# A fused attention and bilinear FFN kernel: up weights in three transfers, and batch 0's two up products in a new order

## The chip, the cores and the metric

The kernel runs on one core of a Trainium2 chip. A core has the engines TensorE (PE, with its weight loads PEld), VectorE (DVE), ScalarE (ACT), GpSimd (POOL) and SyncE (SP), and sixteen DMA engines that all queues share. The time is the device time of one execution in microseconds, here the median of several runs; lower is better.

## What is computed

Eight batches of eight heads, 576 tokens each, head size 64, 32 memory slots. Inputs are float32. The reference, cut to what matters:

```python
a = exp(phi - max(phi over tokens))                 # softmax over the tokens, per memory slot
a = a / (sum(a over tokens) + 1e-9)
k_m = einsum('bhsm,bhsd->bhmd', a, k)               # 32 memory keys and values per head
v_m = einsum('bhsm,bhsd->bhmd', a, v)
attn = softmax(q @ k_m.T / 8)                       # 576 x 32 per head
x = (attn @ v_m), heads side by side                # 4608 tokens x 512
out = ((x @ w_a) * (x @ w_b)) @ w_out               # 512 -> 1536 (two up products) -> 512
```

## The kernel before

**One batch.** The attention output is never formed. For a batch, `sums` (L245) makes the memory keys and values from `exp_sb` (exponentials of phi) and `kv_sb` on TensorE, `transpose` (L269) turns them, `scores` (L279) and `exp_scores` (L301) make E, `denominators` (L308) and `normalise` (L317) make A, the normalised attention. `fold` (L327) multiplies the memory values into a strip of an up weight (w_a is x = 0, w_b is x = 1), and `take_fold` (L345 on) casts the result to `vab`, one half on ACT, one on DVE (L349). An up product is then `vab` times A: `up` (L584) computes for a block i of 128 of the 1536 hidden columns, and for the halves of 288 tokens it is given, first `pa` (L592), which ACT copies to `a_sb` (L595), then `pb` (L602), which DVE multiplies with `a_sb` into `ht` (L605). There are 12 blocks; the first four need columns 0 to 512 of the up weights, and so on. The down product takes `ht` and `wo_sb` into the output.

**Order.** The schedule is written out by hand. A string names units; `chain` (L659) runs one after the other, `ups` (L608) runs up products with units from a second string in the slots between them. `ksN` and `vsN` are sums, `ktN` and `vtN` transposes, `qtN` transposes of q on DVE, `sN`, `eN`, `denN`, `nrN` scores to A, `vNa` and `xNa` fold and cast of strip N of w_a (`b`: w_b), `hv` and `hx` the same for strips of 256 columns. `fN` issues N products of a zero tile of 256 columns, of which nothing is used (`fill`, L147). `yN` issues N products of the first four down tiles (`early_downs`, L408), which read the first third of `wo_sb` in their first 16 products, the second third in the next 16, the last third in the last 16. Batch 0 is L671 to L674, batch 1 L675 to L681; from batch 2 on, the down products run as sums of pairs of token tiles (`two_downs`, L453), for which GpSimd makes `w_sums` once (`sum_weights`, L425) and `h_sums` per pair (L444).

**Loads.** Phi of batch 0 comes on SP's queue and half of its k on ACT's; all other loads are issued by GpSimd in program order, since they cast float32 to float16. The order there: q, k and v of batch 0; the up weights in column strips, w_a and w_b by turns (`load_wab`, L98: strips 0 to 256, 256 to 512, 512 to 1024, 1024 to 1536, called at L157 and L165 to L167); then `wo_sb` in thirds, mixed with phi, k, q and v of batch 1 (L168 to L176); then batches 2 and 3. From the ninth such transfer on, each issue waits for the landing of the transfer eight places before it. GpSimd also computes, so its queue holds arithmetic and issues in one order.

**Buffers.** `a_sb` comes from a pool of four (L48). TensorE's results go to eight PSUM banks, taken in turn (`Banks`, L122).

Of the kernel before, what the change touches and what calls it, by code (L numbers as in the profile page):

```python
# [8 lines left out]
F32 = mybir.dt.float32  # L9
F16 = mybir.dt.float16  # L10
AF = mybir.ActivationFunctionType
ALU = mybir.AluOpType

P = 128
# [4 lines left out]
def kernel(  # L19
# [11 lines left out]
    nc = tc.nc  # L31

    B, H, S, D = q.shape
# [6 lines left out]
    HALF = S // 2  # L40
# [7 lines left out]
    apool = ctx.enter_context(tc.tile_pool(name="apool", bufs=4))  # L48
# [43 lines left out]
    def load(b):  # L92
        load_phi(b)
        load_k(b)
        load_v(b)
        load_q(b)

    def load_wab(lo, hi):  # L98
        nc.gpsimd.dma_start(out=wa_sb[:, :, lo:hi], in_=wa_rows[:, :, lo:hi])
        nc.gpsimd.dma_start(out=wb_sb[:, :, lo:hi], in_=wb_rows[:, :, lo:hi])  # L100
# [6 lines left out]
    ht = consts.tile([P, NFF, 2 * S], F16, name="ht")  # L107
# [37 lines left out]
    banks = Banks()  # L145

    def fill(n, cols=512):  # L147

        pw = banks.tile([P, 512], F32, name="pw")
        for _ in range(n):  # L150
            nc.tensor.matmul(pw[:, :cols], warm[:, :P], warm[:, :cols], start=True, stop=True)
# [2 lines left out]
    make_identity(nc, ident)  # L154
    nc.vector.memset(kv_sbs[0][:, 2], 1.0 / CS)
    nc.vector.tensor_copy(out=kvs[0][:, 0, 0:2], in_=k_f32)
    load_wab(0, 256)  # L157

    ones = consts.tile([P, 4, 32], F16, name="ones")
    nc.vector.memset(ones, 1.0)  # L160
# [1 line left out]
                            pattern=[[-32, 4], [0, 32]], channel_multiplier=1)  # L162
    nc.gpsimd.affine_select(out=ones, in_=ones, compare_op=ALU.is_ge, fill=0.0, base=31,
                            pattern=[[32, 4], [0, 32]], channel_multiplier=-1)
    load_wab(256, 512)  # L165
    load_wab(512, 1024)
    load_wab(1024, 1536)  # L167
    load_wo(0)  # L168
# [10 lines left out]
    attn = {}  # L179
    vabs = {}  # L180
# [237 lines left out]
    KH = NFF // 2  # L418
    NH = d_model // 2
    w_sums = wpool.tile([P, 4, KH, NH], F16, name="w_sums")  # L420

    def quarter(x, y):
        return wo_sb[:, KH * x:KH * (x + 1), NH * y:NH * (y + 1)]

    def sum_weights():  # L425
        t = [w_sums[:, x] for x in range(4)]
        for out, in0, in1 in ((t[0], quarter(0, 1), quarter(0, 0)), (t[1], quarter(1, 1), t[0]),
                              (t[2], quarter(1, 1), quarter(0, 1)), (t[3], quarter(1, 0), t[1])):
            nc.gpsimd.tensor_tensor(out=out, in0=in0, in1=in1, op=ALU.subtract)

    def tokens_of(cidx, x):
        pair, c = divmod(cidx, NI)
# [148 lines left out]

    work = Work()

    def up(b, i, hfs):  # L584
        A, vab = attn[b], vabs[b]
        base = S * (b % 2)
        fs = slice(P * i, P * (i + 1))
        a_sbs = []
        for hf in hfs:
            pa = banks.tile([P, HALF], F32, name="pa")  # L590
            for g in range(2):
                nc.tensor.matmul(pa, vab[0][:, g, fs], A[:, g, HALF * hf:HALF * (hf + 1)],  # L592
                                 start=(g == 0), stop=(g == 1))
            a_sb = apool.tile([P, HALF], F16, name="a_sb")
            nc.scalar.copy(out=a_sb, in_=pa)  # L595
            a_sbs.append(a_sb)
        if len(hfs) > 1:
            yield
        for hf in hfs:
            pb = banks.tile([P, HALF], F32, name="pb")  # L600
            for g in range(2):
                nc.tensor.matmul(pb, vab[1][:, g, fs], A[:, g, HALF * hf:HALF * (hf + 1)],  # L602
                                 start=(g == 0), stop=(g == 1))
            t0 = base + HALF * hf
            nc.vector.tensor_tensor(out=ht[:, i, t0:t0 + HALF], in0=a_sbs[hf - hfs[0]], in1=pb, op=ALU.mult)  # L605
        yield

    def ups(steps, side=()):  # L608

        side = iter(side)  # L610
        for step in steps:
            for _ in up(*step):
                work.advance()
                next(side, us[step[0]]["-"])()
        for f in side:
            work.advance()
            f()

    def steps(b, lo, hi):

        return [(b, i, (0, 1)) for i in range(lo, hi)]
# [14 lines left out]
    def slots(b, names):  # L636

        def both(fs):
            return lambda: [f() for f in fs]
        def unit(n):  # L640
            if n == "fin":
                return lambda: work.pull(-work.done % NFF)
            if n == "L":
                return lambda: load(b + 2) if b + 2 < B else None
            if n[0] == "y":
                return lambda: some(int(n[1:]))
            if n[0] == "d" and n[1:].isdigit():
                return lambda: work.pull(int(n[1:]))
            return us[b + n.endswith("'") - n.endswith("_")][n.rstrip("'_")]

        return [both([unit(n) for n in x.split("+")]) for x in names.split()]
# [3 lines left out]
    def some(n):  # L655
        for _ in range(n):
            next(early, None)

    def chain(b, plan):  # L659


        for x in plan.split():
            if x[0] == "f":
                fill(int(x[1:]), 256)
            elif x[0] == "y":
                some(int(x[1:]))
            else:
                us[b][x]()

    fill(16)  # L670
    chain(0, "exp0 exp1 ks0 kt0 qt0 qt1 f2 s0 e0 ks1 kt1 den0 qt2 qt3 f2 s1 nr0 e1 vs0 vs1 den1 vt0 vt1 nr10 nr11 hv0a hx0a")  # L671
    ups(steps(0, 0, 4), slots(0, "hv0b+hx0b hv1a+hx1a - hv1b+hx1b - v1a+x1a - v1b+x1b"))
    load(2)
    ups(steps(0, 4, 12), slots(0, "- - - - v2a+x2a+v2b+x2b - -"))  # L674
    chain(1, "exp0 exp1 y9 ks0 y3 kt0 qt0 qt1 y1 y3 ks1 qt2 s0 e0 y6 kt1 qt3 den0 y3 s1 nr0 e1 y4 y2 den1 vs0 vs1 vt0 y1 vt1 nr1 hv0a hx0a hv0b y3 hx0b y2")  # L675
    load(3)
    sum_weights()
    ups(steps(1, 0, 4), slots(1, "- hv1a+hx1a hv1b+hx1b+y1 - v1a+x1a y3+v1b x1b y3"))
    ups(half_steps(1, 0, 4), slots(1, "- v2a+x2a+v2b+x2b+qt0' - - qt1'+exp0'+qt2' exp1' - kv'+km'+y9"))
# [43 lines left out]
```

The softmax here doesn't subtract the row's maximum and nothing guards it: scores larger than these inputs give would overflow.

## Time and profile before

| | |
|---|---|
| median of 5 runs | 246.93 us (246.54 to 253.03) |
| the profiled execution | 246.93 us |
| its span, first to last instruction | 245.2 us |
| TensorE busy | 232.0 us (95%), 3016 matmuls |
| VectorE, ScalarE, GpSimd busy | 168.8, 158.2, 154.1 us |
| read from HBM, written | 42.47 MB, 9.44 MB |
| mean granted TensorE clock | 0.984 |

Between the span and the time lie 1.7 us outside the first and last instruction. In the profile's timelines a line has the start, the duration, the engine, the line of the kernel, the operation, what it writes and reads, and the count; in brackets stands the idle time before it and what ended it. Matmuls overlap, so the duration of a group is a little longer than its share of the chain. A DMA issue's duration is that of the issuing instruction, not of the transfer. In the chain of waits a line has a start, a length and what the time went to.

### The profile page before, as it was taken

The page shows a single profiled execution, that of the slowest core. Times are in us where ns is not written, and L with a number is a line of the kernel's source. Part 1 is how long each engine was busy: PE and PEld are TensorE (multiplying, and loading weights), DVE is VectorE, ACT ScalarE, POOL GpSimd, SP SyncE. Part 2 cuts the span into 40 slices and gives each one's busy share as a digit, 9 for nine tenths or more (in the row PEclk, how much of TensorE's full clock was granted, in tenths as well). Part 3 has the DMA queues.
Part 4 walks back from the last instruction along what each step waited for, and adds up shares of the span by engine and source line. Part 5 has one row for each costly group of instructions (what it writes and reads, how often), then busy time and mean ns, then how long its engine had stood idle before and what let it go on. Part 6 is the DMA issues. An engine that isn't in the chain of part 4 may idle for free.

```text
span 245.2 us, 7629 instructions
## 1 busy us (share of the span) xinstructions
PE 232.0 (95%) x3016; PEld 165.1 (67%) x3016; DVE 168.8 (69%) x406; ACT 158.2 (65%) x409; POOL 154.1 (63%) x126
## 2 busy tenths in 40 slices
PE   7579899999998999999999999999999999999993
PEld 2234474456655857677787777877787877888882
DVE  3454883568959958876995549866996576756742
ACT  2365672678697489578855858577856867565330
POOL 8733263399899028892898769892849177937001
PEclk9977999999999999999999999999999999999999
DMA  6999999999979803983059832597030303032154
GB/s 198 211 198 206 207 256 207 255 219 283 224 188 205 169 3 102 234 139 88 17 135 223 192 86 43 151 204 167 21 69 3 86 3 87 4 87 54 43 129 119
DMA packets 26099, 33.81 MB, mean 138 GB/s; under 512 B 1968, under 2 KB 20528, under 8 KB 26064
## 3 DMA queue, kind: packets, MB, share of 16 engines
q0 software_dynamic: 19344, 22.84, 50.8%
q1 hardware_dynamic: 6208, 9.70, 15.9%
q10 hardware_dynamic: 512, 0.79, 0.9%
q8 instruction: 23, 0.38, 0.6%
q14 instruction: 12, 0.10, 0.1%
HBM read 42.47 MB, written 9.44 MB: 212 GB/s over the span
## 4 chain that ended last, share of the span: by engine, by line
PE 82%; DMA 11%; DVE 3%; issue 1%; ACT 1%; POOL 1%; DVEq 0%; POOLq 0%
PE pa L592 19%; PE pb L602 18%; PE py L462 16%; PE pv L462 8%; DMA wb_sb<-in_moe_w_b_dram 6%; PE pva L337 5%; PE po L389 5%; DMA kv_sb<-in_v_dram 4%; PE px L462 4%; PE pkv L213 2%; PE pD L314 2%; PE pscore L292 1%; PE pT L242 1%; PE pk L256 1%; POOL q_sb L90 1%
## 5 line engine op out<-in xcount | busy, mean ns | idle before, releaser
L605 DVE TENSOR_TENSOR ht<-a_sb,pb 128x288 f16<-128x288 f16 x192 | 83.0, 449 | 41.8 <-ACT a_sb L595 28.9
L595 ACT CAST a_sb<-pa 128x288 f16<-128x288 f32 x192 | 75.0, 406 | 31.0 <-PE pa L592 29.0
L592 PE MATMUL pa<-A,vab 128*128 128x288 f16 x384 | 76.8, 288 | 1.5 <-DVE A L325 1.1
L602 PE MATMUL pb<-A,vab 128*128 128x288 f16 x384 | 77.2, 289 | 0.8 <-ACT vab L349 0.6
L444 POOL TENSOR_TENSOR h_sums<-ht 128x768 f16<-128x768 f16 x28 | 45.9, 1642 | 38.2 <-DVE ht L605 37.2
L602 PEld LDWEIGHTS <-vab 128*128 128x128 f16 x384 | 37.4, 99 | 13.8 <-issue 1.7
L592 PEld LDWEIGHTS <-vab 128*128 128x128 f16 x384 | 34.6, 98 | 15.7 <-issue 8.5
L462 PEld LDWEIGHTS <-h_sums 128*128 128x128 f16 x384 | 37.4, 98 | 6.9 <-issue 0.4
L349 ACT CAST vab<-pva 128x512 f16<-128x512 f32 (+1 forms) x52 | 28.1, 559 | 12.5 <-PE pva L337 12.5
L349 DVE CAST vab<-pva 128x512 f16<-128x512 f32 (+1 forms) x52 | 32.7, 644 | 2.8 <-PE pva L337 2.1
L462 PEld LDWEIGHTS <-ht 128*128 128x128 f16 x288 | 28.2, 98 | 5.6 <-issue 0.4
L462 PE MATMUL py<-w_sums,h_sums 128*128 128x256 f16 x192 | 30.3, 272 | 0.0
L444 POOL TENSOR_TENSOR h_sums<-h_sums,ht 128x768 f16<-128x768 f16 x14 | 23.1, 1648 | 0.9
L444 POOL TENSOR_TENSOR h_sums<-ht,h_sums 128x768 f16<-128x768 f16 x14 | 23.0, 1642 | 1.0
L305 ACT ACTIVATE E<-pscore 128x288 f16<-128x288 f32 x32 | 11.4, 417 | 11.3 <-PE pscore L292 11.2
L325 POOL TENSOR_TENSOR A<-E,R 128x576 f16<-128x576 f16 x10 | 12.8, 1278 | 7.0 <-ACT R L323 6.7
L462 PE MATMUL pv<-w_sums,h_sums 128*128 128x256 f16 x96 | 16.0, 273 | 0.0
L462 PE MATMUL py<-wo_sb,ht 128*128 128x256 f16 x96 | 16.0, 273 | 0.0
L469 ACT ACTIVATE u<-py 128x256 f32<-128x256 f32 x32 | 12.4, 388 | 5.2 <-PE py L462 4.9
L462 PE MATMUL py<-w_sums,ht 128*128 128x256 f16 x96 | 15.5, 272 | 0.1
L462 PE MATMUL px<-wo_sb,ht 128*128 128x256 f16 x96 | 15.4, 273 | 0.0
L204 DVE STREAM_TRANSPOSE qT<-q_sb 128x288 f32<-128x288 f32 x32 | 14.3, 463 | 1.2 <-DMA q_sb<-in_q_dram 1.2
(64 smaller groups left out, 263.0 us busy)
## 6 DMA issues: line engine op xcount, KB each, us to landing
out_dram<-o_sb SPq DMA_DIRECT2D x68, 128.0 KB, 2.7
kv_sb<-in_v_dram POOLq DMA_DIRECT2D x7, 576.0 KB, 10.7
phi_sb<-in_phi_dram POOLq DMA_DIRECT2D x7, 576.0 KB, 4.6
kv_sb<-in_k_dram POOLq DMA_DIRECT2D x7, 576.0 KB, 8.6
q_sb<-in_q_dram POOLq DMA_DIRECT2D x6, 576.0 KB, 13.4
wo_sb<-in_moe_w_out_dram POOLq DMA_DIRECT2D x3, 512.0 KB, 16.2
q_sb<-in_q_dram POOLq DMA_DIRECT2D x4, 288.0 KB, 13.1
wa_sb<-in_moe_w_a_dram POOLq DMA_DIRECT2D x2, 512.0 KB, 14.4
```

The source lines that it names most:

```text
L204: nc.vector.transpose(out=t["qT"][:, hp, :].bitcast(F32), in_=qs[b][:, hp, :].bitcast(F32))
L325: engine.tensor_tensor(out=attn[b][:, g, sl], in0=t["E"][:, g, sl], in1=t["R", g][:, sl], op=ALU.mult)
L337: nc.tensor.matmul(t["pva", lo, z][g][0][32 * j:32 * j + 32, 0:hi - lo], t["kvT"][64 * r:64 * r + 64, 4 + g, M * j:M * j + M], w_sbs[z][64 ...
L349: engine_copy(out=vabs[b][z][:, g, lo:hi], in_=pva[:, 0:hi - lo])
L389: nc.tensor.matmul(po, ht[:, i, P * c:P * (c + 1)], wo_sb[:, i, :], start=(i == 0), stop=(i == NFF - 1))
L444: engine.tensor_tensor(out=out, in0=in0, in1=in1, op=op)
L462: nc.tensor.matmul(po, lhs[:, i], rhs[:, i], start=first and i == 0, stop=i == KH - 1, skip_group_check=not first)
L469: nc.scalar.mul(out=x, in_=po, mul=scale)
L592: nc.tensor.matmul(pa, vab[0][:, g, fs], A[:, g, HALF * hf:HALF * (hf + 1)], start=(g == 0), stop=(g == 1))
L595: nc.scalar.copy(out=a_sb, in_=pa)
L602: nc.tensor.matmul(pb, vab[1][:, g, fs], A[:, g, HALF * hf:HALF * (hf + 1)], start=(g == 0), stop=(g == 1))
L605: nc.vector.tensor_tensor(out=ht[:, i, t0:t0 + HALF], in0=a_sbs[hf - hfs[0]], in1=pb, op=ALU.mult)
```

## The change

- The up weights come in three transfers each: strips 0 to 512, 512 to 1024, 1024 to 1536.
- `up` is split into `up_half`, one half of one up product; `chain` gets the names `aI` (both halves of block I with w_a) and `bI` (with w_b). Batch 0 is written as two chains with these names: the `a` products of a strip stand up to four blocks ahead of its `b` products.
- For batch 0, `a_sb` lies in the room of `w_sums`, in 20 places instead of four buffers.
- `w_sums` is made in eight operations of half the size instead of four.
- In the first chain of batch 0, the q transposes and the second key sums move ahead, the scores and the ACT steps change places, the second normalise is one piece, and short fills stand between the steps.

Batch 1 and all that follows keep their strings.

```diff
-    load_wab(0, 256)
+    load_wab(0, 512)
...
-    load_wab(256, 512)
     load_wab(512, 1024)
     load_wab(1024, 1536)
...
-            nc.gpsimd.tensor_tensor(out=out, in0=in0, in1=in1, op=ALU.subtract)
+            for x in range(2):
+                sl = slice(KH // 2 * x, KH // 2 * (x + 1))
+                nc.gpsimd.tensor_tensor(out=out[:, sl], in0=in0[:, sl], in1=in1[:, sl], op=ALU.subtract)
...
+    a_sbs = {}
+    spare = w_sums.rearrange("p x i f -> p (x i f)")
+
+    def up_half(b, i, hf, x):
+        ps = banks.tile([P, HALF], F32, name=("pa", "pb")[x])
+        for g in range(2):
+            nc.tensor.matmul(ps, vabs[b][x][:, g, P * i:P * (i + 1)], attn[b][:, g, HALF * hf:HALF * (hf + 1)],
+                             start=(g == 0), stop=(g == 1))
+        if x == 0:
+            if b == 0:
+                n = (2 * i + hf) % 20
+                a_sbs[b, i, hf] = spare[:, HALF * n:HALF * (n + 1)]
+            else:
+                a_sbs[b, i, hf] = apool.tile([P, HALF], F16, name="a_sb")
+            nc.scalar.copy(out=a_sbs[b, i, hf], in_=ps)
+        else:
+            t0 = S * (b % 2) + HALF * hf
+            nc.vector.tensor_tensor(out=ht[:, i, t0:t0 + HALF], in0=a_sbs.pop((b, i, hf)), in1=ps, op=ALU.mult)
...
+            elif x[0] in "ab":
+                i, _, hf = x[1:].partition(".")
+                for h in ([int(hf)] if hf else (0, 1)):
+                    up_half(b, int(i), h, "ab".index(x[0]))
...
-    chain(0, "exp0 exp1 ks0 kt0 qt0 qt1 f2 s0 e0 ks1 kt1 den0 qt2 qt3 f2 s1 nr0 e1 vs0 vs1 den1 vt0 vt1 nr10 nr11 hv0a hx0a")
-    ups(steps(0, 0, 4), slots(0, "hv0b+hx0b hv1a+hx1a - hv1b+hx1b - v1a+x1a - v1b+x1b"))
+    chain(0, "exp0 exp1 qt0 qt1 f12 ks0 f4 kt0 f2 ks1 f1 s0 e0 kt1 qt2 qt3 f2 den0 f4 s1 e1 nr0 f8 vs0 vs1 den1 f2 vt0 vt1 nr1 f4")
+    chain(0, "v0a x0a f4 a0 a1 v0b x0b f4 b0 b1 a2 b2 v1a x1a a3 b3 a4 a5 v1b x1b a6 a7 b4 b5 v2a x2a b6 b7 a8 a9")
     load(2)
-    ups(steps(0, 4, 12), slots(0, "- - - - v2a+x2a+v2b+x2b - -"))
+    chain(0, "v2b x2b a10 a11 b8 b9 b10 b11")
```

## The prediction

> **What bounds the kernel now.** I read the utilisation slices first, then the chain of waits in order of time, then GpSimd's queue, then single transfers. From the page:
>
> ```profile
> DMA  6999999999979803983059832597030303032154
> ```
>
> Each digit is 6.13 us: the 16 DMA engines are 90% busy or more from 6 us to about 67 us. TensorE is busy too, so both must be followed. The chain of waits:
>
> ```profile
> 3.62 10.71 DMA kv_sb<-in_v_dram
> 14.61 15.76 DMA wb_sb<-in_moe_w_b_dram
> 30.41 0.41 PE pva L337 x8
> 30.82 0.60 PE pb L602 x4
> ...
> 36.31 1.94 PE po L389 x9
> ```
>
> Up to 30.41 the start is a queue of loads; the last part of `wb_sb` ends it. Then 11 groups of up products (six pb, five pa, 0.49 each, 5.49 in all), then batch 1's chain, whose gaps the `po` products fill. So it looks as if moving pa groups ahead of the landing must pay. Whether it does depends on what batch 1 waits for. GpSimd's timeline shows how fast the queue drains, since each issue is released by an earlier landing:
>
> ```profile
> 14.61 0.74 POOL L100 DMA_DIRECT2D wb_sb<-in_moe_w_b_dram  x1 [2.06 <-DMA kv_sb<-in_v_dram]
> 16.78 0.74 POOL L104 DMA_DIRECT2D wo_sb<-in_moe_w_out_dram  x1 [1.43 <-DMA wa_sb<-in_moe_w_a_dram]
> 17.84 0.76 POOL L78 DMA_DIRECT2D phi_sb<-in_phi_dram  x1 [0.31 <-DMA wb_sb<-in_moe_w_b_dram]
> 19.15 0.74 POOL L82 DMA_DIRECT2D kv_sb<-in_k_dram  x1 [0.55 <-DMA wa_sb<-in_moe_w_a_dram]
> 20.48 0.70 POOL L90 DMA_DIRECT2D q_sb<-in_q_dram  x1 [0.59 <-DMA wb_sb<-in_moe_w_b_dram]
> 23.09 0.76 POOL L104 DMA_DIRECT2D wo_sb<-in_moe_w_out_dram  x1 [1.91 <-DMA wa_sb<-in_moe_w_a_dram]
> 25.61 0.70 POOL L90 DMA_DIRECT2D q_sb<-in_q_dram  x1 [1.76 <-DMA wb_sb<-in_moe_w_b_dram]
> 28.11 0.70 POOL L85 DMA_DIRECT2D kv_sb<-in_v_dram  x1 [1.80 <-DMA wa_sb<-in_moe_w_a_dram]
> 30.65 0.71 POOL L85 DMA_DIRECT2D kv_sb<-in_v_dram  x1 [1.84 <-DMA wb_sb<-in_moe_w_b_dram]
> 33.25 0.76 POOL L104 DMA_DIRECT2D wo_sb<-in_moe_w_out_dram  x1 [1.90 <-DMA wo_sb<-in_moe_w_out_dram]
> ```
>
> The releases step by 2.17, 1.06, 1.31, 1.33 us for the four 256 KB parts, then by 2.61, 2.52, 2.50, 2.54, 2.60 for 512 KB: a queue in order at a steady pace. Behind the up weights stand batch 1's loads and the rest of `wo_sb`. Two answers of the trace, for batch 1's k (issued at 19.15) and for the three `wo_sb` transfers (issued at 16.78, 23.09, 33.25):
>
> ```profile
> DMA to landing us min/median/max: 18.6/18.6/18.6
> ```
> ```profile
> DMA to landing us min/median/max: 15.4/16.2/18.6
> ```
>
> So k lands at 19.15 + 18.6 = 37.75. In issue order the three lengths are 16.2, 18.6, 15.4: the first must land shortly before it releases the issue at 33.25, and the last before its use at 48.66. So the second third of `wo_sb` lands at 41.7, the last at 48.65. And TensorE uses them here:
>
> ```profile
> 38.18 0.68 PE L256 MATMUL pk<-kv_sb,exp_sb 64*32 64x128 f16 x36
> 41.75 1.46 PE L389 MATMUL po<-wo_sb,ht 128*128 128x512 f16 x6
> 48.66 1.25 PE L389 MATMUL po<-wo_sb,ht 128*128 128x512 f16 x5
> ```
>
> 0.43, 0.05 and 0.01 us after the landings (these `po` are the 17th and 33rd, the first to read the next third). DVE also waits 1.2 us in its q transposes for q's second half (issued at 25.61). **TensorE's stretch 36 to 48.7 is full, but it already runs at the pace of the loads.** In-order TensorE cannot pass 48.65 earlier than the load queue lets it.
>
> **The change, part by part.** The sum is made against this execution: span 245.2, time 246.93, which is the median shown.
>
> *Three transfers instead of four.* Bytes and order stay. Two issues of 0.75 us leave GpSimd, which idled 0.3 to 2 us before these issues anyway. Each software issue waits for the landing eight places before it, so with two transfers fewer the third strip waits for batch 0's q and k, no longer for its v; it is issued at 10 to 11 us instead of up to 14.61, into a queue that is filled until 30 anyway. Behind it each issue waits for the same data as before or for the strip that ends at the same byte, so the queue stays filled. What can change is the queue's pace. The four 256 KB parts took 5.87 us by releases, two of 512 KB take 2 x 2.54 = 5.08: 0.79 gained at most. But all the excess lies in the first step (2.17), and v's transfer ends in it; the other three average 1.23, less than 2.54 / 2 = 1.27, so leaving the first out the merge would lose 4 x 0.04 = 0.16. The byte rates speak for a middle: 198 to 200 GB/s in the two windows with these parts below, against 206 to 208 in the windows beside them: 3.5% of 8 us, 0.28. I take **0.3**, and keep -0.16 and 0.79. The Trainium skill (DMA: Bandwidth & Descriptors, Anatomy of one DMA) gives each such DMA a fixed 2 us; two fewer would be 4 us. The rows deny it for a filled queue: 256 KB steps are half of 512 KB steps, so no fixed part shows.
>
> *Waiting for whole strips.* The first fold waits until about 17.5 (17.84's release less 0.3) instead of 16.5, its b until 19.9. This lies ahead of the queue's end, where TensorE waited 0.8 for `wb_sb`: nothing, as long as the lead below is positive.
>
> *First chain reordered, 47 short fills for 4, two folds of eight matmuls fewer.* A fill of 256 columns takes half of a 512-column `po` (nine in 1.94): 43 x 0.11 = 4.7 us on TensorE, laid into waits for k, v and the weights. They should keep the clock up, which fell here:
>
> ```profile
> 8.00:12.00 4.00, 2.65 (x98) 1.56 (x98) 1.61 (x6) 1.28 (x4) 3.67 (x7) 1.00 1.21 207
> 12.00:16.00 4.00, 3.58 (x106) 1.87 (x110) 2.39 (x8) 2.18 (x6) 1.29 (x2) 0.57 1.38 198
> 16.00:20.00 4.00, 2.30 (x31) 0.99 (x31) 1.73 (x6) 2.65 (x8) 2.24 (x3) 0.89 1.37 200
> 20.00:24.50 4.50, 4.49 (x43) 2.15 (x41) 2.58 (x7) 2.20 (x6) 1.46 (x2) 0.72 1.25 208
> ```
>
> (After the busy columns: granted clock, DMA share, GB/s.) At half clock 0.57 is 3.4 us, 0.89 and 0.72 together another 3.4. Both spells lie ahead of 30.4, so removing them shortens nothing at the end. Four casts of 256 (0.37 on ACT, 0.42 on DVE) become two of 512 (0.59, 0.68) on each engine, 0.3 less on ACT, 0.3 less on DVE. On DVE the two q transposes (0.83) pass ahead of k's reciprocal, so the scores come about 1 us later, and the last normalise runs whole instead of in two halves (0.69 for 0.78 on ACT); A is done at 17.5 or so either way, because v lands at 14.3 and the weights at 17.5.
>
> *pa ahead of pb.* From the first b (wb landed 19.9, fold 0.41, cast 0.68, start about 21.3) TensorE has 22 groups x 0.49 + four folds x 0.41 = 12.4 us, so 33.7; with 1 us of waits for casts (ACT 0.7 per pa group, DVE 0.82 per pb group plus 0.68 per cast) 34.7. `po` began at 36.15: a lead of 1.4 to 2.4 us at the head of batch 1's chain. It is then given back: k lands 0.3 earlier at 37.45 (used at 38.18: 0.7 left), the second `wo_sb` third at 41.4 (0.3 left), the last at 48.35 (0.3 left). TensorE stands idle for the rest.
>
> *a_sb in w_sums' room.* A copy of the same shape; ACT no longer waits for DVE there. w_sums is written after the last such read, at about 49.9.
>
> *w_sums in eight.* GpSimd's 128x1536 takes 3.10, a 128x768 of the same kind 1.64: 4 x (3.28 - 3.10) = 0.7 more, ending at 62.7 with the 0.3 gained. Its next work, h_sums, started at 63.23 after 0.92 idle for DVE: hidden; uncovered it would cost 0.7.
>
> From 48.66 on the order on every engine is the same, TensorE is 13.36 of 13.40 busy to 62, and batch 2's loads move with the queue. So the sum is the pace alone: 246.93 - 0.3 = **246.6**.
>
> **The rivals.**
> - *The lead survives.* If the landings do not bind (a faster queue, or `po` not held), the 1.4 is kept: 245.5, up to 2.4: 244.5. For it: the chain of waits shows no load after 30.4. Against: three uses within 0.43, 0.05 and 0.01 us of their landings.
> - *The clock falls in batch 1's chain.* TensorE, too early, idles before k (0.7 or more) and before `wo_sb`; a window that is thin in full-size matmuls was followed by a low clock twice above, with 2.65 of 4 and 2.30 of 4 busy. A spell of 3.4 us at half clock takes 1.7 us of work, of which 0.4 to 1.1 falls into idle time: 0.6 to 1.3 slower than the forecast, and a second spell 1.7 more. Take 247.8. It decides if the idle before k passes about 1 us. The Trainium skill (TensorE: Matmul & The Clock Gate, Why this matters for your kernels) asks only that no idle gap pass about 3 us; by that it would not happen. This trace differs: the clock fell with no single wait over 1.1 us (pk for exp_sb).
> - *The split of w_sums shows*, or the queue gains nothing: 246.9 to 247.3.
>
> **How the numbers follow.** Forecast 0.60 (246.1 to 247.1; within it 0.26 below 246.44, 0.34 within 0.2%, about what a measurement here can tell from no change); lead survives 0.16, faster; clock falls 0.17 (0.15 slower, 0.02 within); last 0.07 (0.04 within, 0.03 slower). Faster 0.42, same 0.40, slower 0.18. The range reaches into both rivals: 245.5 to 247.6.
>
> **What would show it.** Right: `po` products (the 17th, 33rd) released by `wo_sb`, idle TensorE before pk near 37 us, the first `po` near 34.7, batch 1's up products 0.3 earlier than 49.75, clock 1.00 from 8 us on. Wrong: the last third of `wo_sb` landing over 0.8 earlier, or a granted clock under 1 between 36 and 50.

## The result and the profile after

| | before | changed |
|---|---|---|
| median of all runs shown | 247.1 us (246.28 to 253.33, 53 runs) | 246.35 us (246.09 to 247.0, 28 runs) |
| the profiled execution, its span | 246.93, 245.2 us | 245.99, 244.3 us |
| TensorE busy, matmuls | 232.0 us, 3016 | 232.9 us, 3043 |
| VectorE, ScalarE, GpSimd busy | 168.8, 158.2, 154.1 us | 167.8, 157.2, 153.2 us |
| mean granted clock | 0.984 | 0.998 |

The ratio is 0.9973, 95% interval [0.9967, 0.9978]: 0.67 us faster, and 246.35 lies 0.25 below the 246.6 forecast. Four runs of before (252.38 to 253.33) stand apart from the rest; the ratio leaves them out.

The chain of waits of the changed kernel (start, length, what the time went to):

```profile
8.00 14.87 DMA wa_sb<-in_moe_w_a_dram
...
23.15 17.56 DMA wo_sb<-in_moe_w_out_dram
...
40.75 1.46 PE po L388 x6
```

Before, the last load in this chain ended at 30.37 and TensorE carried nearly all that followed. Now one transfer, the second third of `wo_sb`, carries it from 23.15 to 40.71 (17.56 long). The chain changed its look much and its end little. TensorE's timeline shows why (start, duration; in brackets the idle time before and what ended it):

```profile
34.15 2.11 PE L388 MATMUL po<-wo_sb,ht 128*128 128x512 f16 x9
36.87 0.68 PE L255 MATMUL pk<-kv_sb,exp_sb 64*32 64x128 f16 x36 [0.61 <-DMA kv_sb<-in_k_dram]
40.75 1.46 PE L388 MATMUL po<-wo_sb,ht 128*128 128x512 f16 x6 [0.26 <-DMA wo_sb<-in_moe_w_out_dram]
47.66 1.25 PE L388 MATMUL po<-wo_sb,ht 128*128 128x512 f16 x5
```

The first `po` starts 2.0 us earlier than before (34.15 for 36.15), the 17th (third row) 1.0, the 33rd (last row) 1.0. Half of the lead is gone after two waits for loads that did not show before. The windows of the start (busy time of PE, PEld, DVE, ACT, POOL, then granted clock, DMA share, GB/s):

```profile
8.00:12.00 4.00, 3.25 (x94) 1.70 (x83) 2.40 (x9) 0.73 (x3) 3.74 (x6) 1.00 1.21 206
12.00:16.00 4.00, 2.67 (x82) 1.77 (x82) 1.21 (x4) 2.00 (x5) 0.76 (x1) 1.00 1.24 207
16.00:20.00 4.00, 3.66 (x56) 2.06 (x55) 1.70 (x5) 2.46 (x6) 0.74 (x1) 1.00 1.25 207
```

Against before's rows: the clock is full where it was 0.57 and 0.89, and the loads run at 207 GB/s where the 256 KB strips had held them at 198 and 200.

### The profile page after: what moved, and what is told of

Same layout as the page of the kernel before. It is cut to its first block, busy times and chain, and to the rows that moved or that the text cites. A ratio compares the mean times of both kernels' runs of the same rounds, so it can differ in the third digit from the quotient of the medians.

```text
span 244.3 us, 7659 instructions
## 1 busy us (share of the span) xinstructions
PE 232.9 (95%) x3043; PEld 167.5 (69%) x3043; DVE 167.8 (69%) x403; ACT 157.2 (64%) x406; POOL 153.2 (63%) x128
## 4 chain that ended last, share of the span: by engine, by line
PE 78%; DMA 16%; DVE 3%; ACT 1%; issue 1%; POOL 0%; DVEq 0%
PE pa L591 18%; PE py L463 17%; PE pb L591 17%; PE pv L463 8%; DMA wo_sb<-in_moe_w_out_dram 7%; DMA wa_sb<-in_moe_w_a_dram 6%; PE pva L336 5%; PE px L463 4%; PE po L388 3%; DMA ht<-in_k_dram 2%; PE pkv L212 2%; PE pD L313 2%; PE pscore L291 1%; PE pT L241 1%; DVE A L324 1%
## 5 line engine op out<-in xcount | busy, mean ns | idle before, releaser
L602 DVE TENSOR_TENSOR ht<-a_sb,pb 128x288 f16<-128x288 f16 x168 | 73.2, 449 | 38.1 <-ACT a_sb L599 29.2
L599 ACT CAST a_sb<-pa 128x288 f16<-128x288 f32 x168 | 66.4, 406 | 28.0 <-PE pa L591 26.1
L591 PE MATMUL pa<-A,vab 128*128 128x288 f16 x384 | 75.8, 287 | 1.4 <-DVE A L324 1.1
L591 PE MATMUL pb<-A,vab 128*128 128x288 f16 x384 | 75.0, 286 | 0.3 <-ACT vab L348 0.3
L314 ACT ACTIVATE L<-pD 128x288 f32<-128x288 f32 x32 | 11.5, 418 | 5.0 <-PE pD L313 4.7
```

Of the source, the lines that this page charges most:

```text
L314: nc.scalar.activation(out=t["L", g][:, sl], in_=pD, func=AF.Ln)
L591: nc.tensor.matmul(ps, vabs[b][x][:, g, P * i:P * (i + 1)], attn[b][:, g, HALF * hf:HALF * (hf + 1)], start=(g == 0), stop=(g == 1))
L599: nc.scalar.copy(out=a_sbs[b, i, hf], in_=ps)
```

## The experiments

**The theories.** They are named as in the expectations below. A: in the kernel before, the load queue and TensorE reach the second third of `wo_sb` together, so moving one alone gains little; in the changed kernel batch 1's chain starts early, is stopped by the landings of k and of that third, and ends as the queue allows. B: the shorter queue is the whole gain. C: the order of the products is the whole gain.

### Loads alone, and all but the merged strips

The first kernel is the one before with the strips merged, all else as before (the first four blocks use the same data from the larger strip). The second is the changed kernel with its four transfers back:

```diff
-    load_wab(0, 256)
+    load_wab(0, 512)
...
-    load_wab(256, 512)
```
```diff
-    load_wab(0, 512)
+    load_wab(0, 256)
+    load_wab(256, 512)
```

> The kernel before, with the up weights in three transfers and nothing else changed. Theory A (two things end together: the load queue and TensorE reach the second third of wo_sb within 0.05 us of each other in the kernel before, so neither an earlier queue nor an earlier TensorE gains alone): TensorE still begins the po products near 36.2 and reaches the 17th near 41.7, time within 0.2 us of before. Theory B (the shorter queue is the whole gain): 0.5 to 0.8 us faster. Theory C (the order of the products is the whole gain): as before.

> The changed kernel with its up weights in four transfers each again; order and fills kept. Theory A: TensorE has its lead (first po near 34.2) and waits for k and wo_sb; the gain is what the queue allows, so 0.2 to 0.5 us slower than the changed kernel (the four smaller parts run 3.5% slower over 8 us: 0.28). Theory B: no gain left, as before (0.7 slower than the changed kernel). Theory C: as fast as the changed kernel (0.7 faster than before).

Loads alone: three of nine runs lie at 247.05 to 247.43 (before, run beside it, has a median of 247.07), no gain. The other six lie at 250.29 to 253.75, where theory A wanted all within 0.2 of before; the ratio of 1.0067 [1.0023, 1.011] holds two of them. The trace is of one of the three: TensorE had no wait for a load in batch 1's chain, and its 17th `po` started at 42.21, 0.46 later than in before and 0.87 behind the landing at 41.34. So in these runs the earlier landings have no taker, against B; the six long runs have no trace. Four strips: 246.68 (246.33 to 247.48), ratio 0.9992 [0.9981, 1.0003], 0.33 above the changed kernel. Its timeline of TensorE:

```profile
37.65 0.68 PE L256 MATMUL pk<-kv_sb,exp_sb 64*32 64x128 f16 x36 [0.33 <-DMA kv_sb<-in_k_dram]
41.48 1.46 PE L389 MATMUL po<-wo_sb,ht 128*128 128x512 f16 x6 [0.21 <-DMA wo_sb<-in_moe_w_out_dram]
```

The same two waits stand there, 0.73 later at the 17th `po` than in the changed kernel's trace. Merging is worth 0.33 by the medians and 0.47 by the ratios when the order lets TensorE use it. C falls as the sole cause: with the order, chain and fills but without the merge, 0.2 (by the ratio) to 0.39 (by the medians) is left, and the ratio's interval reaches no change.

### The products in pairs

The changed kernel with batch 0's `a` and `b` products of a block next to each other, loads, fills and first chain kept:

```diff
-    chain(0, "v0a x0a f4 a0 a1 v0b x0b f4 b0 b1 a2 b2 v1a x1a a3 b3 a4 a5 v1b x1b a6 a7 b4 b5 v2a x2a b6 b7 a8 a9")
+    chain(0, "v0a x0a f4 a0 v0b x0b f4 b0 a1 b1 a2 b2 v1a x1a a3 b3 v1b x1b a4 b4 a5 b5 a6 v2a x2a")
...
-    chain(0, "v2b x2b a10 a11 b8 b9 b10 b11")
+    chain(0, "v2b x2b b6 a7 b7 a8 b8 a9 b9 a10 b10 a11 b11")
```

> The changed kernel with batch 0's products in pairs (pa, pb of one block, as before); three transfers, new first chain and fills kept. Theory A: TensorE begins po near 36 and arrives at the 17th po near 41.6, after the data: within 0.2 us of before, 0.5 to 0.7 slower than the changed kernel. Theory B: as fast as the changed kernel. Theory C: as before.

246.8 (246.68 to 247.09), ratio 0.9992 [0.9983, 1.0]: 0.45 slower than the changed kernel (A expected 0.5 to 0.7). TensorE waited 1.3 us for the last `wb_sb` strip, its first `po` came at 35.88 and the 17th at 41.47, with `wo_sb` there since 40.81. So without `a` ahead of `b` TensorE itself is the later one again, and the rest of the change (merge, first chain, fills, with the clock at 1.00 from 8 us on) gains about 0.2 to 0.27 instead of 0.67 to 0.75. The three kernels together say: **before ends at the later of two nearly equal things**, TensorE and the load queue; moving one alone gains 0 to 0.4, moving both 0.67.

### A useless load ahead of batch 1's loads, and one behind them

One line in the changed kernel, a 256 KB cast load into a part of `ht` that is overwritten before it is read, either right after the last up weights or after the last third of `wo_sb`:

```diff
     load_wab(1024, 1536)
+    nc.gpsimd.dma_start(out=ht[:, 8:12, S:S + 256], in_=wa_rows[:, :, 0:256])
```

> The changed kernel with one useless load of 256 KB put into the queue behind the up weights, ahead of wo_sb and batch 1's loads (it writes a part of ht that batch 1 writes over later). If the landings of k and wo_sb set the time (theory A), every landing behind it comes 1.25 us later (half of a 512 KB step of 2.5) and the time is 1.0 to 1.3 us longer than the changed kernel's. If TensorE's lead sets it (theory C), TensorE waits longer in batch 1's chain but ends within 0.3 us.

> The same useless 256 KB, but behind the last third of wo_sb, ahead of batch 2's loads. Theory A: the landings up to wo_sb stay; batch 2's q lands 1.25 us later where it had 0.6 us to spare, so 0 to 0.7 us longer than the changed kernel. A rival, that the bytes in the start as a whole set the time: 1.0 to 1.3 us longer, as with the load put ahead.

Ahead: nine of fourteen runs lie at 247.56 to 248.15, their median 247.64, **1.3 slower than the changed kernel for 1.27 us of queue** (half of a 512 KB step of 2.54); the ratio to before is 1.0027 [1.0014, 1.004]. What the queue loses, the end loses, as A says; which landing passes it on has to be read from waits. The other five runs lie at 262.6 to 264.5, and the profiled execution is one of them. It shows the rival that the prediction had named. TensorE's timeline, then the windows 38.5 to 42.7 and 42.7 to 48:

```profile
38.56 0.68 PE L256 MATMUL pk<-kv_sb,exp_sb 64*32 64x128 f16 x36 [2.16 <-DMA kv_sb<-in_k_dram]
39.18 1.42 PE L389 MATMUL po<-wo_sb,ht 128*128 128x512 f16 x3
```
```profile
38.50:42.70 4.20, 4.14 (x55) 1.39 (x56) 1.49 (x5) 0.00 (x0) 1.48 (x2) 0.59 1.22 206
42.70:48.00 5.30, 5.30 (x95) 2.42 (x95) 1.99 (x6) 2.71 (x7) 2.24 (x3) 1.00 1.21 237
```

TensorE waited 2.16 for k, and the clock fell right behind it: three `po` took 1.42 for the usual 0.82, and 0.59 over 4.2 us is 4.2 x 0.41 x 2 = 3.4 us at half clock. The long runs have a mean granted clock of 0.965 to 0.974, the nine others 0.999 or 1.0. But 3.4 us at half clock are not 15 to 17 us; the rest is the subject of the next experiment.

Behind: 247.92 (247.69 to 249.77), ratio 1.0047 [1.0025, 1.007], 1.57 slower. I had expected 0 to 0.7 and missed; the number lies nearer to the rival named there, that the bytes of the start as a whole set the time. DVE's timeline at batch 2's start shows which landing took it:

```profile
60.70 0.48 DVE L204 STREAM_TRANSPOSE qT<-q_sb 128x288 f32<-128x288 f32 x1 [1.44 <-DMA q_sb<-in_q_dram]
```

Batch 2's q had landed 0.48 before its use in the changed kernel's trace (58.32 for 58.80), 0.58 in before's. It is the third landing with next to no spare, and with a load in front it binds. A load ahead delays this q as well, so the 1.3 alone does not tell batch 1's landings from it; the wait of 2.16 for k does, in the one execution traced. The next test asked whether batch 2's q binds as the kernel stands.

### Batch 2's q ahead of its v

```diff
         load_k(b)
-        load_v(b)
-        load_q(b)
+        if b == 2:
+            load_q(b)
+            load_v(b)
+        else:
+            load_v(b)
+            load_q(b)
```

> The changed kernel with batch 2's q loaded ahead of its v (nothing else moved). DVE takes this q at 59.2 within 0.5 us of its landing, v is read at 60.7 or later. If that landing is the third place where the queue binds: q lands about 2.8 us earlier, v still in time, and the time falls by 0.1 to 0.5 us against the changed kernel (245.9 to 246.2). If it doesn't bind: within 0.1 us.

246.41 (246.27 to 246.5), ratio 0.9966 [0.9954, 0.9978]. Q landed at 56.17, two us earlier, and nothing came of it: no gain where I had expected up to 0.5. (In one other trace, of `w_sums` in four below, DVE does wait 0.18 for this q.) So that landing is close but sets no time here; what binds lies further ahead, where TensorE in this trace too waits 1.01 for k and 0.26 for `wo_sb`.

### No fills

The changed kernel without its 47 short fills (all `fN` taken out of the two strings of batch 0):

```diff
-    chain(0, "exp0 exp1 qt0 qt1 f12 ks0 f4 kt0 f2 ks1 f1 s0 e0 kt1 qt2 qt3 f2 den0 f4 s1 e1 nr0 f8 vs0 vs1 den1 f2 vt0 vt1 nr1 f4")
-    chain(0, "v0a x0a f4 a0 a1 v0b x0b f4 b0 b1 a2 b2 v1a x1a a3 b3 a4 a5 v1b x1b a6 a7 b4 b5 v2a x2a b6 b7 a8 a9")
+    chain(0, "exp0 exp1 qt0 qt1 ks0 kt0 ks1 s0 e0 kt1 qt2 qt3 den0 s1 e1 nr0 vs0 vs1 den1 vt0 vt1 nr1")
+    chain(0, "v0a x0a a0 a1 v0b x0b b0 b1 a2 b2 v1a x1a a3 b3 a4 a5 v1b x1b a6 a7 b4 b5 v2a x2a b6 b7 a8 a9")
```

> The changed kernel without the 47 short fills of batch 0. Theory A: the clock falls again between 8 and 24 us, 3.4 to 6.8 us at half speed; that takes 1.7 to 3.4 us of TensorE work from a lead of 2.0 us at the first po. With one low spell the time stays within 0.2 us of the changed kernel, with two it is near that of before. Rival (fills only delay): 0 to 0.3 us faster than the changed kernel, clock above 0.95 throughout.

262.35 (261.75 to 263.0), ratio 1.0618 [1.0603, 1.0634]: **16 us slower, which no theory had**. Two things show. First, the clock: granted 0.52, 0.50 and 0.83 in 16 to 20, 20 to 24.5 and 24.5 to 30, and the first `po` at 37.21 for 34.15:

```profile
16.00:20.00 4.00, 3.07 (x75) 1.28 (x61) 1.98 (x6) 2.03 (x5) 1.41 (x2) 0.52 1.24 206
20.00:24.50 4.50, 3.79 (x22) 1.91 (x21) 1.76 (x4) 2.13 (x5) 1.46 (x2) 0.50 1.24 207
```

Second, and far larger, this (the timeline of all engines at batch 1's up products):

```profile
49.24 13.91 DVE L324 TENSOR_TENSOR A<-E,R 128x576 f16<-128x576 f16 x1
49.30 0.75 POOL L90 DMA_DIRECT2D q_sb<-in_q_dram  x1
50.06 3.25 POOL L430 TENSOR_TENSOR w_sums<-wo_sb 128x768 f16<-128x768 f16 x2
...
63.54 0.90 PE L591 MATMUL pa<-A,vab 128*128 128x288 f16 x3 [12.45 <-DVE vab L348]
```

The second A product of batch 1 takes 13.91 us; in the changed kernel it takes 0.45, from 47.18 on, 1.71 ahead of GpSimd's `w_sums`:

```profile
47.18 0.45 DVE L324 TENSOR_TENSOR A<-E,R 128x576 f16<-128x576 f16 x1
48.89 3.25 POOL L430 TENSOR_TENSOR w_sums<-wo_sb 128x768 f16<-128x768 f16 x2
```

Without fills it starts only 0.82 ahead, and it ends at 63.15, 0.32 behind the last of GpSimd's eight `w_sums` operations. DVE stands for the whole row, so the casts of `vab` behind it wait, and TensorE idles 12.45; in that idle time the clock falls once more (0.69 in 48.6 to 62). The long execution of the useless load shows the same: product at 50.12, 13.89 us long, `w_sums` from 50.93.

Reading: GpSimd's operations on SBUF shut out a DVE product with both inputs in SBUF. GpSimd itself loses nothing (3.25 us for two operations in both kernels), and in the changed kernel DVE's products with one input in PSUM, `ht<-a_sb,pb`, take 0.82 for two beside the same row, as they do before it. Two kernels test it. If it is the row of operations that holds DVE, four operations that wait on each other should let DVE in between. If it is the nearness, a GpSimd copy of two columns ahead of `w_sums` that reads the product's result, and so waits for it, should cure it. Each is the kernel without fills with one edit more:

```diff
-            for x in range(2):
-                sl = slice(KH // 2 * x, KH // 2 * (x + 1))
-                nc.gpsimd.tensor_tensor(out=out[:, sl], in0=in0[:, sl], in1=in1[:, sl], op=ALU.subtract)
+            nc.gpsimd.tensor_tensor(out=out, in0=in0, in1=in1, op=ALU.subtract)
```
```diff
     def sum_weights():
+        nc.gpsimd.tensor_copy(out=w_sums[:, 0, 0, 0:2], in_=attn[1][:, 1, S - 2:S])
```

> The changed kernel without the fills and with w_sums in four operations instead of eight. In the run without fills DVE's last product for A of batch 1 took 13.9 us instead of 0.45, from just before GpSimd's w_sums to just after them. If GpSimd's row of operations shuts DVE out (both read SBUF), and lets it in only where one of them waits for the one before: 3 to 7 us slower than before (250 to 254) instead of 15, that product 3.5 to 7 us long. If something else holds that product (a late R, a semaphore): 262 again.

> The changed kernel without the fills, and with one tiny GpSimd copy ahead of w_sums that reads the end of A of batch 1, so that w_sums can't start before DVE has finished it. If the 15 us were GpSimd's row of operations shutting DVE out, that product takes 0.45 us again and the time is what the lost lead costs: the first po came at 37.2 instead of 36.15 in before, so 247.5 to 248.3. If the fills matter in another way, it stays above 250.

Four operations: 252.61 (251.82 to 253.51), ratio 1.0228 [1.0203, 1.0253].

```profile
49.33 4.24 DVE L324 TENSOR_TENSOR A<-E,R 128x576 f16<-128x576 f16 x1
50.13 3.10 POOL L428 TENSOR_TENSOR w_sums<-wo_sb 128x1536 f16<-128x1536 f16 x1
53.32 3.19 POOL L428 TENSOR_TENSOR w_sums<-wo_sb,w_sums 128x1536 f16<-128x1536 f16 x1
```

DVE is let in after the first operation, which ends at 53.23, and is done 0.34 later. With the guard: 248.59 (247.75 to 249.1), ratio 1.005 [1.0032, 1.0067].

```profile
49.90 0.45 DVE L324 TENSOR_TENSOR A<-E,R 128x576 f16<-128x576 f16 x1
50.69 0.20 POOL L425 COPY w_sums<-A 128x2 f16<-128x2 f16 x1
50.98 3.23 POOL L431 TENSOR_TENSOR w_sums<-wo_sb 128x768 f16<-128x768 f16 x2
```

The product is back at 0.45 us, and 13.8 of the 16 us are gone. What is left, 2.2 over the changed kernel (my range ended 0.3 below it), is, as far as the trace shows, the price of the clock (TensorE waits for nothing in it from 36 to 62): granted 0.79, 0.50, 0.50, 0.69 in the windows from 12 to 30, about 13.6 us at half clock, first `po` at 37.87, the 17th at 43.46.

The Trainium skill (SBUF — State Buffer, Who interferes with whom) says that a VectorE instruction with two inputs in SBUF contends with a GpSimd instruction that reads SBUF. Its words on the lock, "Whoever issues first gets the shared pair for the whole instruction", stand there beside other VectorE modes, but it also says without such a limit that the order of issue decides who blocks; by that DVE, which started first by the records, should have won, or lost one operation of 1.6 us. The traces show DVE losing eight in a row. Why a product of 0.45 us that starts 0.80 to 0.82 ahead of `w_sums`, and so should be over 0.35 before it, is caught, while one 0.87 ahead (loads alone) is not, stays open. The profile's GpSimd times are rough; between the two lies GpSimd's issue of q, which alone does no harm (the guard kernel has it at the same place).

The shut-out stands in small in both kernels of this document. The changed kernel's last A product of batch 2:

```profile
72.38 1.46 DVE L324 TENSOR_TENSOR A<-E,R 128x576 f16<-128x576 f16 x1
```

A GpSimd `h_sums` operation runs from 71.85 to 73.51, the next one, which reads its result, starts at 73.59, and the product ends at 73.84, again 0.33 behind the first. The kernel before has the same 1.46 at 73.38, and in both traces TensorE waits 1.1 us for this A. So before's profile held the warning.

### w_sums in four operations, fills kept

The changed kernel with the first of the last two diffs alone, fills in place.

> The changed kernel with w_sums in four operations, all else kept. The split costs GpSimd 0.5 us by the profile (12.9 for 12.4), which ends 0.5 us ahead of h_sums' start: hidden, so within 0.1 us of the changed kernel. Rival (the split gives DVE gaps, and is part of the gain): 0.3 us or more slower, or runs above 249.

246.34 (245.93 to 246.61), ratio 0.9973 [0.996, 0.9985], that of the changed kernel. The split into eight costs and brings nothing here; it only makes the shut-out 13.9 long instead of 4.24 if it happens.

### Both kernels once more

Each kernel again unchanged, for another trace of the same moments:

> The kernel before, for a second trace. If the distance between the first and the last of the 16 engines' landings (2.6 us at the second third of wo_sb, 1.8 in the changed kernel) belongs to the execution and not to the kernel, it may differ here by some tenths; the fastest engine's landing should be the same within 0.1 us.

> The changed kernel, for a second trace. The wait of TensorE for k (0.61 us) and for wo_sb (0.26) come again within 0.3 us, the second third of wo_sb lands between 40.7 and 41.1, and DVE may wait for batch 2's q.

Before came out at 246.85. Its TensorE:

```profile
41.65 1.47 PE L389 MATMUL po<-wo_sb,ht 128*128 128x512 f16 x6
```

The second third of `wo_sb` had landed at 41.37: 0.28 to spare, where the first trace had 0.04. The last third had 0.31 (48.26 for 48.57), where the first had 0.04. The changed kernel came out at 246.71, with 0.92 of idle before pk, 0.26 before the 17th `po` at 41.29, and the 33rd at 48.38:

```profile
37.41 0.68 PE L255 MATMUL pk<-kv_sb,exp_sb 64*32 64x128 f16 x36 [0.92 <-DMA kv_sb<-in_k_dram]
```

This pair of traces differs by 0.36 and 0.19 at those two places where the first pair differed by 1.0. The cause can be seen in the landings of the single DMA engines, of which a trace records 16 per transfer. The fastest of the 16 finishes the second third of `wo_sb` at 39.08 to 39.22 in the three traces with four strips and at 38.87 to 38.94 in ten traces with three: 0.25 earlier, always. The slowest follows 1.8 to 2.6 later, differently in each execution (before 2.63 and 2.15, changed 1.81 and 2.36 in the two pairs), and the wait lasts for the slowest. Of the expectations, the wait for `wo_sb` came again and DVE did not wait for batch 2's q. Three missed narrowly: the wait for k differed by 0.31 (0.3 allowed), that landing came at 41.25 (41.1 at the latest), and before's fastest engine differed by 0.14 (0.1 allowed).

No experiment gave a version that is faster than the changed kernel: q ahead of v and `w_sums` in four lie within 0.1 of it.

## Why the prediction was right, and where it was off

- **The queue sets the pace; the lead is given back.** Right. First `po` at 34.15 and 34.38 in the two traces (34.7 said; lead 2.0 in the first, within 1.4 to 2.4), idle before k 0.61 and 0.92 (0.7), wait for `wo_sb` 0.26 twice (0.3). The wait that was expected before the 33rd `po` is small: it starts 0.06 and 0.04 behind the landing, with no idle time marked. Batch 1's up products start at 48.75 and 49.46 (0.3 earlier than 49.75 said). The waits for k and `wo_sb` come back in every trace that has the new order of the products, its fills and no useless load; the useless load ahead, 1.3 for 1.27, agrees with them but does not prove it alone, since the load behind costs as much. The rival *the lead survives* is out.
- **The merge, 0.3.** Right: 0.33 by the medians and 0.47 by the ratios between four strips and the changed kernel; the fastest engine says 0.25. The fixed 2 us per DMA, which the prediction quotes from the Trainium skill (DMA: Bandwidth & Descriptors, Anatomy of one DMA), do not show.
- **The order gains nothing of its own.** This is the term that was too small: "From 48.66 on the order on every engine is the same ... So the sum is the pace alone." With the merge taken out, 0.2 to 0.39 is left where the prediction had nothing. I had taken TensorE's spare before `wo_sb`, 0.05 and 0.01 (0.04 and 0.04 by the records of the landings, not rounded), from one execution; a second shows 0.28 and 0.31. So in part of the executions TensorE was probably the later one, by about as much as the order gained; two traces don't show how often. 0.3 + 0.3 would have been 246.3. The forecast held because its range was wider than this term.
- **"Removing them shortens nothing at the end"**, of the spells of low clock. Right for before's order, where a wait for `wb_sb` covers them; wrong as a statement on the fills. In the new order 13.6 us at half clock put the first `po` at 37.87 and cost 2.2. The fills are what lets the lead be there at all.
- **The clock falls in batch 1's chain.** It did not: the window from 36 to 48.6 has 1.00, and idle times of 0.61 and 0.92, and 1.01 in the kernel with q ahead, were not enough. "It decides if the idle before k passes about 1 us" was near: at 2.16 it fell, and 5 of 14 runs of that kernel were long; in the nine others the clock stayed at 0.999 or 1.0. Its price of 0.6 to 1.3 was some ten times too small, since in the long run that was traced the delay brought the shut-out with it. The 2.16 us also lie below the idle gap of about 3 us of the rule that the prediction cites (Trainium skill, TensorE: Matmul & The Clock Gate, Why this matters for your kernels): the measurement decides against the rule.
- **w_sums in eight.** Hidden, as said; 12.84 us for 12.40, 0.44 more where 0.7 was said, ending at 61.73 with `h_sums` still 0.50 idle behind it. What nobody had: it stands 1.7 us from a DVE product that it can hold for 13.9 us.
- **The last third of `wo_sb` landing over 0.8 earlier** was named as what would be wrong. It landed 1.02 earlier in the first pair of traces (47.60 for 48.62) and 0.08 later in the second (48.34 for 48.26). One execution on each side could not carry that test.

**Open.** What before's few runs above 251 and those of loads alone above 250 are: their excess of 3 to 7 us is about that of one or two of four `w_sums` operations (3.1 us each) holding DVE, but none of them was traced. And why the nearness of 0.8 us decides.

## What to carry to other kernels

Where two limits end within a few tenths of each other, take each one's spare from several executions and expect little from moving one alone; a useless load in the queue shows by its own length that some landing behind it binds, and the waits in its trace show which. Work that only warms TensorE can be worth its time when it lies in waits, and is judged by the kernel without it. Before a VectorE product with two SBUF inputs is moved near a row of GpSimd operations, look at the distance between them: the profile shows it as a single operation of several times its usual length (1.46 for 0.45 us in the kernel before, 13.91 without fills), and a GpSimd operation of a few columns that waits for the product removes it.

## What was not expected of the hardware

- A 128x576 product on DVE took 13.91 us instead of 0.45 beside eight gapless GpSimd operations, 4.24 beside four that wait on each other, and 0.45 again ahead of the guard.
- The clock fell in spells of 3.41 us or a multiple of it: 3.41 twice and 6.83 in the two traces of before, 10.24 without fills, 13.65 with the guard. Those of before came with no single wait over 1.1 us, at 12 to 24.5 in one trace (0.57, 0.89, 0.72) and at 16 to 24.5 in another (0.68, 0.53): the place changes from execution to execution.
- The slowest of the 16 DMA engines ends the same transfer 1.8 to 2.6 us behind the fastest, and that lag, unlike the fastest's landing, changes with each execution.
